# Two blocks' first layer as seven products of parts (Strassen) in an fp32 feed-forward kernel behind a state-space scan

## Chip, cores and metric

The kernel runs on one core of a Trainium2 chip. The metric is the device time of one execution in microseconds. A core has TensorE (matrix products, into PSUM), VectorE, ScalarE and GpSimd (elementwise work) and DMA queues. The profile calls them PE (PEld is its weight load), DVE, ACT and POOL. PSUM has 8 banks of 128 partitions x 512 fp32.

## The reference, cut to what matters

A Mamba2 scan (4 batches, 8 heads, 768 tokens, head size 32) makes y; y is laid out as 3072 tokens x 256, and a feed-forward layer with ELU follows. All is fp32.

```python
x = attn_out.transpose(0, 2, 1, 3).reshape(B * S, H * D)   # 3072 x 256
h = x @ w_in                                                # w_in 256 x 2048
g = np.where(h > 0.0, h, np.exp(np.minimum(h, 0.0)) - 1.0)
return g @ w_out                                            # w_out 2048 x 256
```

## The kernel before

The 3072 tokens are 12 blocks of 256 (`NP = 12`). Block n's scan result stands transposed in `yT[n // 2]`, two blocks in a tile, in two parts of 128 rows (`KC = 2`). `w_in` is cut into 16 column groups of 128 (`MC = 16`). The scan of blocks further on is spread between the products of the feed-forward layer. The instructions of each engine stay in the order of the program (`manual_schedule`); the framework adds the waits and gives out the buffers.

The pools in PSUM: seven banks for everything but the second layer's sums, one bank for those.

```python
p_a = ctx.enter_context(tc.tile_pool(name="ps_a", bufs=7, space=PSUM))
p_o = ctx.enter_context(tc.tile_pool(name="ps_o", bufs=1, space=PSUM))
def psum(shape, name):
    return p_a.tile(shape, F32, tag="a", name=name)
```

A step of the first layer makes two column groups, h of 128 x 2 x 256, with four products. The ELU takes three passes: Relu and Exp on ScalarE, then max(e - 1, h) on VectorE, which also frees the bank.

```python
def l1(n, i):
    if i == 0:
        g_of[n] = ffn.tile([P, MC, BLK], F32, tag="g", name="g", bufs=3)
    ps = psum([P, 2, BLK], "ps_h")
    for j in range(2):
        m = 2 * i + j
        for k in range(KC):
            nc.tensor.matmul(
                out=ps[:, j], lhsT=w_in[:, k, m * P:(m + 1) * P],
                rhs=yT[n // 2][:, k, n % 2].rearrange("p u i -> p (u i)"),
                start=(k == 0), stop=(k == KC - 1))
    lag.append((n, i, ps))

def elu():
    n, i, ps = lag.pop(0)
    e = ffn.tile([P, 2, BLK], F32, tag="e", name="e", bufs=3)
    nc.scalar.activation(e, ps, ACT.Relu, scale=-1.0)
    nc.scalar.activation(e, e, ACT.Exp, scale=-1.0)
    nc.vector.scalar_tensor_tensor(
        out=g_of[n][:, 2 * i:2 * i + 2], in0=e, scalar=1.0, in1=ps,
        op0=ALU.subtract, op1=ALU.max)
```

A step of the second layer, `l2(n, j)`, adds two of the 16 column groups for both halves of the block's tokens, four products as well, into the bank `ps_o` of block n. The last step copies the bank to SBUF with ScalarE and writes it out.

The scan's parts that take PSUM banks from `p_a`: `turn` two (`ps_tb`, `ps_tc`), `scores` four (`ps_g`), which `weigh` reads on VectorE one bank after another; `sums` two (`ps_st`), which `states` reads on VectorE; `across` and `inside` four (`ps_y`), which ScalarE copies into `yT`. `decay` is ScalarE work.

```python
def scores(*ns):
    gs = [psum([P, len(ns), 2, 2, Q], "ps_g") for _ in range(4)]
    # ... 32 products a block; gs[q] for q = 0..3 in turn

def sums(*ns, pool=p_a, tag="a", parts=(None, None)):
    ps = [psum([P, len(ns), 2, 2 * D], "ps_st"),
          pool.tile([P, len(ns), 2, 2 * D], F32, tag=tag, name="ps_st")]
    # ... 16 products a block
```

The loop from block 2 on, cut:

```python
ends = {(3, 14): 4, (5, 8): 6, (7, 13): 8, (9, 6): 10}
def end_of_two(n, step):
    m = ends.get((n, step))
    if m:
        inside(across(m, m + 1), m, m + 1)

for n in range(2, NP):
    for i in range(8):
        l2(n - 2, i)
        # ... conversion of further weights while there are any
        end_of_two(n, 2 * i)
        l1(n, i)
        while lag:
            elu()
        # ... scan of block 3
        m = n + 2 - n % 2
        if 4 <= m < NP and n % 2 == 0:
            # ... loads; decay (i >= 2); turn, turn_exp (i == 5, 7)
        if 4 <= m < NP and n % 2 == 1:
            # ... scaled (i == 0), decay (i < 2)
            if i == (1 if m in (6, 10) else 2):
                scores(m, m + 1)
                sums(m, m + 1)
                for q in range(4):
                    weigh(m, q)
                    weigh(m + 1, q)
                states(m)
                states(m + 1)
        end_of_two(n, 2 * i + 1)
for i in range(8):
    l2(NP - 2, i)
l2_last(NP - 1)
```

Of the kernel before, what the change touches and what calls it, by code (L numbers as in the profile page):

```python
# [10 lines left out]
F32 = mybir.dt.float32  # L11
# [17 lines left out]
def kernel(  # L29
# [43 lines left out]
    ffn = ctx.enter_context(tc.tile_pool(name="ffn", bufs=2))  # L73
    conv = ctx.enter_context(tc.tile_pool(name="conv", bufs=2))
    PSUM = bass.MemoryType.PSUM
    p_a = ctx.enter_context(tc.tile_pool(name="ps_a", bufs=7, space=PSUM))
    p_o = ctx.enter_context(tc.tile_pool(name="ps_o", bufs=1, space=PSUM))

    def psum(shape, name):
        return p_a.tile(shape, F32, tag="a", name=name)  # L80
# [21 lines left out]
    def rows_of(n):  # L102
        b, g = place(n)
        return slice(NG * NH * b + g, NG * NH * (b + 1), NG)
# [101 lines left out]

    idle = att.tile([P, P], BF16, tag="M", name="idle", bufs=8)
    nc.vector.memset(idle, 0.0)  # L210
    ps_idle = p_o.tile([P, 4, P], F32, tag="o", name="ps_idle")

    def idle_products(count):
        for _ in range(count):
            nc.tensor.matmul(
                out=ps_idle, lhsT=idle, rhs=idle.unsqueeze(1).to_broadcast([P, 4, P]),
                start=True, stop=True)

    def idle_product(k):

        nc.tensor.matmul(
            out=ps_idle[:, 0:k], lhsT=ident, rhs=ident.unsqueeze(1).to_broadcast([P, k, P]),
            start=True, stop=True)

    idle_products(7)
    ident = const.tile([P, P], F32, name="ident")
    make_identity(nc, ident)

# [28 lines left out]
        out=minus, in0=ident, scalar1=-1.0, scalar2=None, op0=ALU.mult)  # L257


    heads = [const.tile([ROWS, NH, N], F32, name=f"heads{n}") for n in range(2)]  # L260
    heads.append(heads[0])

    def make_heads(n):
        rows, cols = (slice(BH, 2 * BH), slice(BH + NH * n, BH + NH * (n + 1))) if n < 2 else (
            slice(0, ROWS), rows_of(n))
        count = rows.stop - rows.start
        nc.gpsimd.tensor_copy(
            heads[n][rows], ident[rows, cols].unsqueeze(2).to_broadcast([count, NH, N]))

    make_heads(0)  # L270
    make_heads(1)
# [84 lines left out]
    def first_exp(n):  # L356

        ps = psum([P, 2, P], "ps_ec")
        rows = slice(BH, 2 * BH) if n < 2 else slice(0, ROWS)
        nc.tensor.matmul(  # L360
            out=ps, lhsT=heads[n][rows].rearrange("p h n -> p (h n)"),
            rhs=X0 if n < 2 else F[:, 1], start=True, stop=True,
            tile_position=(rows.start, 0))
        st[n]["ec"] = att.tile([P, 2, P], F32, tag="ec", name="ec", bufs=4)
        nc.scalar.copy(out=st[n]["ec"], in_=ps)

# [183 lines left out]
    def inside(y, *ns):  # L550


        for t in range(2):
            if t and ns[0] == 0:
                idle_products(1)
            for at, n in enumerate(ns):
                s = st[n]
                for u in range(2):
                    for v in range(2):
                        toks = slice(Q * v, Q * v + Q)  # L560
                        for q in range(4):
                            h, col = 4 * t + q, (D * q + shift(n, v)) % P
                            nc.tensor.matmul(  # L563
                                out=y[t][v][col:col + D, at, u],
                                lhsT=s["x"][toks, u, D * h:D * (h + 1)],
                                rhs=s["M"][h // 2][toks, u, h % 2], start=False, stop=True,
                                tile_position=(Q * v, col), skip_group_check=True)
            n = ns[0]
            if n // 2 not in yT:
                yT[n // 2] = ffn.tile([P, KC, 2, 2, P], F32, tag="yT", name="yT")  # L570
            out = yT[n // 2][:, t, n % 2:n % 2 + len(ns)]
            for v in range(2):
                k = shift(n, v)
                for at in (0, k) if k else (0,):
                    count, src = P - k, (at + k) % P
                    to, src = out[at:at + count, :, :, Q * v:Q * v + Q], y[t][v][src:src + count]
                    if t and n == 1:
                        nc.vector.tensor_copy(to, src)
                    else:
                        nc.scalar.copy(out=to, in_=src)  # L580
        for n in ns:
            st.pop(n)
# [3 lines left out]

    def l1(n, i):

        if i == 0:
            g_of[n] = ffn.tile([P, MC, BLK], F32, tag="g", name="g", bufs=3)  # L590
        ps = psum([P, 2, BLK], "ps_h")
        for j in range(2):
            m = 2 * i + j
# [6 lines that stand above are left out]

    lag = []

    def elu():

        n, i, ps = lag.pop(0)
        e = ffn.tile([P, 2, BLK], F32, tag="e", name="e", bufs=3)
        nc.scalar.activation(e, ps, ACT.Relu, scale=-1.0)  # L607
        nc.scalar.activation(e, e, ACT.Exp, scale=-1.0)  # L608
        nc.vector.scalar_tensor_tensor(  # L609
            out=g_of[n][:, 2 * i:2 * i + 2], in0=e, scalar=1.0, in1=ps,  # L610
            op0=ALU.subtract, op1=ALU.max)

    def row_of(n):
        b, g = place(n)
# [4 lines left out]
    def l2(n, j):  # L619


        if j == 0:
            o_of[n] = p_o.tile([P, 2, DM], F32, tag="o", name="ps_o")
        for m in (2 * j, 2 * j + 1):
            for ts in range(2):
                nc.tensor.matmul(  # L626
                    out=o_of[n][:, ts], lhsT=g_of[n][:, m, ts * P:(ts + 1) * P],
                    rhs=w_out[:, m], start=(m == 0 and ts == 0), stop=(m == MC - 1),
                    skip_group_check=True)
        if j == MC // 2 - 1:  # L630
            ob = ffn.tile([P, 2, DM], F32, tag="ob", name="ob")
            nc.scalar.copy(out=ob, in_=o_of.pop(n))  # L632
            r0 = row_of(n)
            nc.sync.dma_start(
                out=out[r0:r0 + BLK, :].rearrange("(t p) e -> p t e", p=P), in_=ob)

    def l2_last(n):

        for ts in range(2):
            ps = psum([P, DM], "ps_o")  # L640
            for m in range(MC):
                nc.tensor.matmul(  # L642
                    out=ps, lhsT=g_of[n][:, m, ts * P:(ts + 1) * P], rhs=w_out[:, m],
                    start=(m == 0), stop=(m == MC - 1))
            ob = ffn.tile([P, 2, DM], F32, tag="ob", name="ob")
            nc.scalar.copy(out=ob[:, ts], in_=ps)
            r0 = row_of(n) + ts * P
            nc.sync.dma_start(out=out[r0:r0 + P, :], in_=ob[:, ts])
# [50 lines left out]
    w_abs(1)  # L699
    kept = st[0]  # L700
    inside(across(0), 0)
    idle_product(3)
    w_low(1, nc.scalar)

    w_sign(1)
# [96 lines left out]
    def end_of_two(n, step):  # L802
        m = ends.get((n, step))
        if m:
            inside(across(m, m + 1), m, m + 1)


    for n in range(2, NP):
        for i in range(8):
            l2(n - 2, i)  # L810
            if todo < len(pieces):
# [9 lines left out]
            if n == 2:  # L821
# [11 lines left out]
                if i == 4:  # L833
                    sums(3)
                    states(3)
            if n == 2 and i == 6:
                inside(across(3), 3)

            m = n + 2 + n % 2
            if 4 < m < NP and n % 2 == 1 and i in (4, 5):  # L840
                spread_cum(m + i - 4)
            m = n + 2 - n % 2
            if 4 <= m < NP and n % 2 == 0:
                if i < 2:
                    if m == 4:
                        spread_cum(m + i)
                    load_bc(m + i)
                    spread_exp(m + i)
                if i == 2:
                    load_x(m)  # L850
                    load_x(m + 1)
                if i >= 2:
                    decay(m + i // 6, (i - 2) % 4)
                if i in (5, 7):
                    turn(m + i // 7)
                    turn_exp(m + i // 7)
            if 4 <= m < NP and n % 2 == 1:
                if i == 0:
                    scaled(m, nc.gpsimd)
                    scaled(m + 1, nc.gpsimd)  # L860
                if i < 2:
                    decay(m + 1, i + 2)
                if i == (1 if m in (6, 10) else 2):
                    scores(m, m + 1)
                    sums(m, m + 1)
                    for q in range(4):
                        weigh(m, q)
                        weigh(m + 1, q)
                    states(m)
                    states(m + 1)  # L870
            end_of_two(n, 2 * i + 1)
    for i in range(8):
        l2(NP - 2, i)
    l2_last(NP - 1)
# [30 lines left out]
```

## Time and profile before

| | |
|---|---|
| device time, median of 3 | 387.46 us (387.11 to 388.42) |
| span of the profiled execution | 385.5 us |
| TensorE busy | 380.4 us |
| ScalarE busy | 197.1 us |
| VectorE busy | 142.7 us |
| GpSimd busy | 73.8 us |
| first layer, `l1` (L595) | 768 records, 181.9 us |
| second layer, `l2` (L626) and `l2_last` (L642) | 704 and 64 records, 166.0 and 14.0 us |

The page gives first the busy time of each engine, then the chain of work that ended last, then the groups of instructions: line, engine and operation, output and inputs, shapes, count, busy time and mean duration of one, and the idle time of the engine just before them with what ended it. A timeline row is start, duration, engine, line, operation and count; rows of one kind that follow each other are merged. The durations of pipelined matmuls overlap, so the price of one is the distance between starts.

### The profile page before, as it was taken

The page shows a single profiled execution, that of the slowest core. Times are in us where ns is not written, and L with a number is a line of the kernel's source. Part 1 is how long each engine was busy: PE and PEld are TensorE (multiplying, and loading weights), DVE is VectorE, ACT ScalarE, POOL GpSimd, SP SyncE. Part 2 cuts the span into 40 slices and gives each one's busy share as a digit, 9 for nine tenths or more (in the row PEclk, how much of TensorE's full clock was granted, in tenths as well). Part 3 has the DMA queues.
Part 4 walks back from the last instruction along what each step waited for, and adds up shares of the span by engine and source line. Part 5 has one row for each costly group of instructions (what it writes and reads, how often), then busy time and mean ns, then how long its engine had stood idle before and what let it go on. Part 6 is the DMA issues. An engine that isn't in the chain of part 4 may idle for free.

```text
span 385.5 us, 8722 instructions
## 1 busy us (share of the span) xinstructions
PE 380.4 (99%) x3568; PEld 324.5 (84%) x3568; DVE 142.7 (37%) x289; ACT 197.1 (51%) x458; POOL 73.8 (19%) x134
## 2 busy tenths in 40 slices
PE   8999999999999999999999999999999999999996
PEld 5668888888888888888888888888888888888885
DVE  3989978932511232611133431124422212221000
ACT  4859969675344576344467335367444333334000
POOL 4554527624100112300022120011310000000000
PEclk9999999999999999999999999999999999999999
DMA  8968987555014505003425001640000000000000
GB/s 170 220 162 208 242 202 146 92 103 111 2 28 55 84 2 136 3 3 61 65 38 130 10 0 35 68 66 29 2 4 0 27 2 26 1 2 28 2 27 27
DMA packets 96248, 25.24 MB, mean 65 GB/s; under 512 B 77328, under 2 KB 92112, under 8 KB 96208
## 3 DMA queue, kind: packets, MB, share of 16 engines
q1 hardware_dynamic: 94032, 24.49, 30.7%
q8 instruction: 28, 0.46, 0.5%
q10 hardware_dynamic: 2176, 0.20, 0.4%
q14 instruction: 12, 0.10, 0.1%
HBM read 21.33 MB, written 3.34 MB: 64 GB/s over the span
## 4 chain that ended last, share of the span: by engine, by line
PE 93%; DVE 4%; ACT 1%; POOL 1%; DMA 1%; issue 0%; ACTq 0%; DVEq 0%; POOLq 0%
PE ps_h L595 41%; PE ps_o L626 40%; PE ps_o L642 4%; PE ps_y L563 2%; PE ps_g L467 2%; PE ps_y L542 1%; PE ps_st L497 1%; DVE mag L183 1%; DVE mag L190 1%; PE ps_tb L382 1%; PE ps_tc L382 1%; DMA la<-in_a_dram 1%; DVE M L476 1%; DVE sgn L175 0%; DVE F L281 0%; POOL w_in L200 0%
## 5 line engine op out<-in xcount | busy, mean ns | idle before, releaser
L595 PE MATMUL ps_h<-yT,w_in 128*128 128x256 f32 x768 | 181.9, 381 | 0.8 <-DVE sgn L175 0.4
L626 PE MATMUL ps_o<-w_out,g 128*128 128x256 f32 x704 | 166.0, 380 | 0.0
L595 PEld LDWEIGHTS ps_h<-yT,w_in 128*128 128x128 f32 x768 | 144.8, 190 | 22.9 <-POOL w_in L200 1.9
L626 PEld LDWEIGHTS ps_o<-w_out,g 128*128 128x128 f32 x704 | 132.4, 190 | 18.1 <-POOL L L452 0.2
L609 DVE SCALAR_TENSOR_TENSOR g<-e,ps_h 128x512 f32<-128x512 f32 x96 | 65.7, 686 | 203.5 <-ACT e L608 203.5
L607 ACT ACTIVATE e<-ps_h 128x512 f32<-128x512 f32 x96 | 57.0, 594 | 134.3 <-PE ps_h L595 130.1
L608 ACT ACTIVATE e<-e 128x512 f32<-128x512 f32 x96 | 60.5, 630 | 3.1
L452 POOL TENSOR_SCALAR_AFFINE_SELECT L<-L 64x512 f32<-64x512 f32 x40 | 27.3, 684 | 158.4 <-ACT L L447 157.1
L447 ACT ACTIVATE L<-L,ncum 128x64 f32<-128x64 f32 x160 | 42.1, 332 | 0.3 <-DMA L<-flat 0.3
L580 ACT COPY yT<-ps_y 64x256 f32<-64x256 f32 (+3 forms) x43 | 13.6, 321 | 11.7 <-PE ps_y L563 11.2
L476 DVE TENSOR_TENSOR M<-ps_g,L 128x256 f32<-128x256 f32 x48 | 17.0, 415 | 0.4 <-PE ps_g L467 0.3
L519 POOL TENSOR_TENSOR Sx<-S_new,hmask 128x64 f32<-128x64 f32 x44 | 12.8, 302 | 17.0 <-DVE S_new L514 11.9
L632 ACT COPY ob<-ps_o 128x512 f32<-128x512 f32 x11 | 6.4, 578 | 15.3 <-PE ps_o L626 15.3
L642 PE MATMUL ps_o<-w_out,g 128*128 128x256 f32 x64 | 14.0, 379 | 0.0
L200 POOL TENSOR_TENSOR w_in<-mag,w_in 128x512 uint32<-128x512 uint32 (+1 forms) x9 | 11.3, 1253 | 13.6 <-DVE mag L190 10.6
L642 PEld LDWEIGHTS ps_o<-w_out,g 128*128 128x128 f32 x64 | 12.2, 190 | 1.7
L200 POOL TENSOR_TENSOR w_out<-mag,w_out 128x512 uint32<-128x512 uint32 x8 | 10.2, 1276 | 14.4 <-DVE mag L190 14.4
L190 DVE SCALAR_TENSOR_TENSOR mag<-mag,sgn 128x512 uint32<-128x512 uint32 (+1 forms) x17 | 12.3, 722 | 0.6
L157 ACT ACTIVATE mag<-w 128x512 f32<-128x512 f32 x16 | 10.8, 676 | 1.9 <-POOL w_in L200 0.9
L514 DVE SCALAR_TENSOR_TENSOR S_new<-S_new,ec,ps_st 128x64 f32<-128x64 f32 x40 | 10.9, 279 | 2.0
L183 DVE TENSOR_SCALAR mag<-mag 128x512 f32<-128x512 f32 (+1 forms) x17 | 10.3, 606 | 1.0 <-ACT mag L157 1.0
L563 PE MATMUL ps_y<-M,xr 64*32 64x64 f32 x768 | 9.8, 225 | 0.0
(74 smaller groups left out, 141.7 us busy)
## 6 DMA issues: line engine op xcount, KB each, us to landing
L<-flat SPq DMA_DIRECT2D x20, 256.0 KB, 5.0
w<-in_moe_w_in_dram SPq DMA_DIRECT2D x8, 512.0 KB, 5.3
w<-in_moe_w_out_dram SPq DMA_DIRECT2D x8, 512.0 KB, 5.8
xr<-in_x_dram SPq DMA_DIRECT2D x24, 128.0 KB, 3.5
out_dram<-ob SPq DMA_DIRECT2D x11, 256.0 KB, 2.2
bc<-in_B_dram SPq DMA_DIRECT2D x24, 64.0 KB, 3.5
bc<-in_C_dram SPq DMA_DIRECT2D x22, 64.0 KB, 2.9
ec<-flat_exp SPq DMA_DIRECT2D x72, 16.0 KB, 1.7
```

What stands on the lines that cost most here:

```text
L190: nc.vector.scalar_tensor_tensor(out=mag, in0=mag, scalar=3, in1=sgn, op0=ALU.logical_shift_left, op1=ALU.bitwise_xor)
L200: nc.gpsimd.tensor_tensor(out=w, in0=w_mag[i][:, :, cols], in1=w, op=ALU.add)
L447: nc.scalar.activation(L[:, h, u], L[:, h, u], ACT.Exp, bias=ncum[:, u, row:row + 1])
L452: nc.gpsimd.affine_select(out=part, in_=part, pattern=[[0, 4], [0, 2], [1, Q]], compare_op=ALU.is_ge, fill=0.0, base=0, channel_multiplier=-1)
L476: nc.vector.tensor_tensor(out=M, in0=s["g"][q], in1=s["L"][:, 2 * q:2 * q + 2].rearrange("p k u i -> p u k i"), op=ALU.mult)
L563: nc.tensor.matmul(out=y[t][v][col:col + D, at, u], lhsT=s["x"][toks, u, D * h:D * (h + 1)], rhs=s["M"][h // 2][toks, u, h % 2], start=Fal ...
L595: nc.tensor.matmul(out=ps[:, j], lhsT=w_in[:, k, m * P:(m + 1) * P], rhs=yT[n // 2][:, k, n % 2].rearrange("p u i -> p (u i)"), start=(k = ...
L607: nc.scalar.activation(e, ps, ACT.Relu, scale=-1.0)
L608: nc.scalar.activation(e, e, ACT.Exp, scale=-1.0)
L609: nc.vector.scalar_tensor_tensor(out=g_of[n][:, 2 * i:2 * i + 2], in0=e, scalar=1.0, in1=ps, op0=ALU.subtract, op1=ALU.max)
L626: nc.tensor.matmul(out=o_of[n][:, ts], lhsT=g_of[n][:, m, ts * P:(ts + 1) * P], rhs=w_out[:, m], start=(m == 0 and ts == 0), stop=(m == MC ...
L642: nc.tensor.matmul(out=ps, lhsT=g_of[n][:, m, ts * P:(ts + 1) * P], rhs=w_out[:, m], start=(m == 0), stop=(m == MC - 1))
```

## The change

From block 4 on, two blocks n and n + 1 go together. For them and two column groups of `w_in` the first layer is a product of a 2 x 2 matrix of parts (128 x 128 of `w_in`) with a 2 x 2 matrix of parts (128 x 256 of `yT`). Done part by part that takes eight products. Strassen's algorithm, here in the form with fifteen sums, takes seven, with sums of weight parts, of input parts and of results around them. The aim is one product less on TensorE for each of the 32 steps (four pairs of blocks, eight steps each).

The sums of weight parts are made once on GpSimd during block 3 (`sum_weights`), those of the inputs once for each pair on GpSimd (`sum_y`). A step is cut in two: `front` makes four products and, after a copy by ScalarE, three sums on VectorE; `back` adds three products into the same two PSUM banks, and VectorE adds once to each bank. The result is h of both blocks in `c1` and `c2`, and the ELU follows for each. Between `front` and `back`, and ahead of `front`, stands one step of the second layer: steps of blocks n - 2 and n - 1 alternate, so two banks hold second-layer sums, and the pool of the others has six.

```diff
-    p_a = ctx.enter_context(tc.tile_pool(name="ps_a", bufs=7, space=PSUM))
-    p_o = ctx.enter_context(tc.tile_pool(name="ps_o", bufs=1, space=PSUM))
+    p_a = ctx.enter_context(tc.tile_pool(name="ps_a", bufs=6, space=PSUM))
+    p_o = ctx.enter_context(tc.tile_pool(name="ps_o", bufs=2, space=PSUM))
...
+    def begin_elu():
+        begun.append(ffn.tile([P, 2, BLK], F32, tag="e", name="e", bufs=3))
+        nc.scalar.activation(begun[0], lag[0][2], ACT.Relu, scale=-1.0)
...
+    def front(n, i):
+        c1, c2 = psum([P, 2, BLK], "ps_h"), psum([P, 2, BLK], "ps_h")
+        s1, s2, s3, s4 = (w[:, i] for w in w_sums)
+        t = y_sums[n]
+        part_product(c1[:, 0], a11[:, i], yT[n // 2][:, 0, 0].rearrange("p u i -> p (u i)"), True)
+        part_product(c2[:, 1], s2, t[:, 1], True)
+        part_product(c2[:, 0], s1, t[:, 0])
+        part_product(c1[:, 1], s3, t[:, 2])
+
+        copy = conv.tile([P, BLK], F32, tag="sgn", name="p_copy")
+        nc.scalar.copy(out=copy, in_=c1[:, 0])
+        u = conv.tile([P, 2, BLK], F32, tag="mag", name="u_sum")
+        nc.vector.tensor_tensor(out=u[:, 0], in0=c2[:, 1], in1=copy, op=ALU.add)
+        nc.vector.tensor_tensor(out=u[:, 1], in0=c2[:, 0], in1=u[:, 0], op=ALU.add)
+        nc.vector.tensor_tensor(out=c2[:, 1], in0=c1[:, 1], in1=u[:, 1], op=ALU.add)
+        open_[n, i] = c1, c2, u
+
+    def back(n, i):
+        c1, c2, u = open_.pop((n, i))
+        b21, b22 = (yT[n // 2][:, 1, at].rearrange("p u i -> p (u i)") for at in range(2))
+        part_product(c1[:, 0], a12[:, i], b21)
+        part_product(c1[:, 1], a22[:, i], y_sums[n][:, 3])
+        part_product(c2[:, 0], w_sums[3][:, i], b22)
+        nc.vector.tensor_tensor(out=c1[:, 1], in0=c1[:, 1], in1=u[:, 0], op=ALU.add)
+        nc.vector.tensor_tensor(out=c2[:, 0], in0=c2[:, 0], in1=u[:, 0], op=ALU.add)
+        lag.append((n, i, c1))
+        lag.append((n + 1, i, c2))
...
-    for n in range(2, NP):
+    for n in (2, 3):
         # ... as before, with sum_weights(i) in block 3
+    for n in range(4, NP, 2):
+        for k in range(16):
+            l2(n - 2 + k % 2, k // 2)
+            at = n + k // 8
+            end_of_two(at, 2 * (k % 8))
+            if k % 2 == 0:
+                front(n, k // 2)
+            else:
+                back(n, k // 2)
+            if lag:
+                elu()
+            if lag:
+                begin_elu()
+            scan_ahead(at, k % 8)
+            end_of_two(at, 2 * (k % 8) + 1)
+    while lag:
+        elu()
```

`elu` takes up a Relu that `begin_elu` has issued. `scan_ahead` is the part of the old loop that works on the scan of the next blocks, unchanged. `end_of_two` also calls `sum_y(m)`. The outputs g get 24 small buffers for three large ones.

Smaller edits go with it. The products on zeros that fill TensorE at the start are fp32, one over 4 x 128 and one over 3 x 128 columns, in place of seven in bf16 over 512; two such fillings further on, one inside the first `inside` and one behind it, are gone. `heads` and the product in `first_exp` take all 128 rows for the first two blocks where they took 32.

More of the change, by code (lines that the diff above doesn't have):

```diff
@@ L205 @@
     w_load(0)
-    idle = att.tile([P, P], BF16, tag="M", name="idle", bufs=8)
+    idle = att.tile([P, P], F32, tag="M", name="idle", bufs=8)
     nc.vector.memset(idle, 0.0)
     ps_idle = p_o.tile([P, 4, P], F32, tag="o", name="ps_idle")
[L213 to L217, printed above, removed]
     def idle_product(k):
         nc.tensor.matmul(
-            out=ps_idle[:, 0:k], lhsT=ident, rhs=ident.unsqueeze(1).to_broadcast([P, k, P]),
+            out=ps_idle[:, 0:k], lhsT=idle, rhs=idle.unsqueeze(1).to_broadcast([P, k, P]),
             start=True, stop=True)
-    idle_products(7)
+    idle_product(4)
+    idle_product(3)
     ident = const.tile([P, P], F32, name="ident")
@@ L257 @@
         out=minus, in0=ident, scalar1=-1.0, scalar2=None, op0=ALU.mult)
-    heads = [const.tile([ROWS, NH, N], F32, name=f"heads{n}") for n in range(2)]
+    heads = [const.tile([P, NH, N], F32, name=f"heads{n}") for n in range(2)]
     heads.append(heads[0])
     def make_heads(n):
-        rows, cols = (slice(BH, 2 * BH), slice(BH + NH * n, BH + NH * (n + 1))) if n < 2 else (
-            slice(0, ROWS), rows_of(n))
-        count = rows.stop - rows.start
+        cols = slice(BH + NH * n, BH + NH * (n + 1)) if n < 2 else rows_of(n)
         nc.gpsimd.tensor_copy(
-            heads[n][rows], ident[rows, cols].unsqueeze(2).to_broadcast([count, NH, N]))
+            heads[n], ident[:, cols].unsqueeze(2).to_broadcast([P, NH, N]))
     make_heads(0)
@@ L358, in first_exp @@
         ps = psum([P, 2, P], "ps_ec")
-        rows = slice(BH, 2 * BH) if n < 2 else slice(0, ROWS)
+        rows = P if n < 2 else ROWS
         nc.tensor.matmul(
-            out=ps, lhsT=heads[n][rows].rearrange("p h n -> p (h n)"),
-            rhs=X0 if n < 2 else F[:, 1], start=True, stop=True,
-            tile_position=(rows.start, 0))
+            out=ps, lhsT=heads[n][0:rows].rearrange("p h n -> p (h n)"),
+            rhs=la0 if n < 2 else F[:, 1], start=True, stop=True)
         st[n]["ec"] = att.tile([P, 2, P], F32, tag="ec", name="ec", bufs=4)
@@ L553, in inside @@
         for t in range(2):
-            if t and ns[0] == 0:
-                idle_products(1)
             for at, n in enumerate(ns):
@@ L587, in l1 @@
     def l1(n, i):
-        if i == 0:
-            g_of[n] = ffn.tile([P, MC, BLK], F32, tag="g", name="g", bufs=3)
         ps = psum([P, 2, BLK], "ps_h")
@@ L601 @@
     lag = []
+    begun = []
+    def begin_elu():
+        begun.append(ffn.tile([P, 2, BLK], F32, tag="e", name="e", bufs=3))
+        nc.scalar.activation(begun[0], lag[0][2], ACT.Relu, scale=-1.0)
     def elu():
+        if not begun:
+            begin_elu()
         n, i, ps = lag.pop(0)
-        e = ffn.tile([P, 2, BLK], F32, tag="e", name="e", bufs=3)
-        nc.scalar.activation(e, ps, ACT.Relu, scale=-1.0)
+        e = begun.pop()
         nc.scalar.activation(e, e, ACT.Exp, scale=-1.0)
+        g_of[n, i] = ffn.tile([P, 2, BLK], F32, tag="g", name="g", bufs=24)
@@ L609, in elu, with sum_weights @@
         nc.vector.scalar_tensor_tensor(
-            out=g_of[n][:, 2 * i:2 * i + 2], in0=e, scalar=1.0, in1=ps,
+            out=g_of[n, i], in0=e, scalar=1.0, in1=ps,
             op0=ALU.subtract, op1=ALU.max)
+    w_parts = w_in.rearrange("p k (i r c) -> p k r i c", r=2, c=P)
+    a11, a12, a21, a22 = (w_parts[:, k, r] for r in range(2) for k in range(2))
+    w_sums = []
+    def sum_weights(step):
+        r, part = step // 2, slice(4 * (step % 2), 4 * (step % 2) + 4)
+        if step % 2 == 0:
+            w_sums.append(conv.tile([P, MC // 2, P], F32, tag="w64", name="w_sum", bufs=W_AHEAD))
+        in0, in1, op = (
+            (a21, a22, ALU.add), (w_sums[0], a11, ALU.subtract),
+            (a11, a21, ALU.subtract), (a12, w_sums[min(r, 1)], ALU.subtract))[r]
+        nc.gpsimd.tensor_tensor(out=w_sums[r][:, part], in0=in0[:, part], in1=in1[:, part], op=op)
@@ new lines, with sum_y, part_product @@
+    y_sums = {}
+    def sum_y(n):
+        t = y_sums[n] = conv.tile([P, 4, BLK], F32, tag="w64", name="y_sum", bufs=W_AHEAD)
+        b11, b12, b21, b22 = (
+            yT[n // 2][:, k, at].rearrange("p u i -> p (u i)") for k in range(2) for at in range(2))
+        for r, (in0, in1) in enumerate(((b12, b11), (b22, t[:, 0]), (b22, b12), (b21, t[:, 1]))):
+            nc.gpsimd.tensor_tensor(out=t[:, r], in0=in0, in1=in1, op=ALU.subtract)
+    open_ = {}
+    def part_product(out, lhsT, rhs, first=False):
+        nc.tensor.matmul(
+            out=out, lhsT=lhsT, rhs=rhs, start=first, stop=True, skip_group_check=True)
@@ L626, in l2 @@
                 nc.tensor.matmul(
-                    out=o_of[n][:, ts], lhsT=g_of[n][:, m, ts * P:(ts + 1) * P],
+                    out=o_of[n][:, ts], lhsT=g_of[n, j][:, m % 2, ts * P:(ts + 1) * P],
                     rhs=w_out[:, m], start=(m == 0 and ts == 0), stop=(m == MC - 1),
@@ L642, in l2_last @@
                 nc.tensor.matmul(
-                    out=ps, lhsT=g_of[n][:, m, ts * P:(ts + 1) * P], rhs=w_out[:, m],
+                    out=ps, lhsT=g_of[n, m // 2][:, m % 2, ts * P:(ts + 1) * P], rhs=w_out[:, m],
                     start=(m == 0), stop=(m == MC - 1))
@@ L701 @@
     inside(across(0), 0)
-    idle_product(3)
     w_low(1, nc.scalar)
@@ L805, in end_of_two, with scan_ahead @@
             inside(across(m, m + 1), m, m + 1)
-    for n in range(2, NP):
+            sum_y(m)
+    def scan_ahead(n, i):
+        m = n + 2 + n % 2
+        if 4 < m < NP and n % 2 == 1 and i in (4, 5):
+            spread_cum(m + i - 4)
+        m = n + 2 - n % 2
+        if 4 <= m < NP and n % 2 == 0:
+            if i < 2:
+                if m == 4:
+                    spread_cum(m + i)
+                load_bc(m + i)
+                spread_exp(m + i)
+            if i == 2:
+                load_x(m)
+                load_x(m + 1)
+            if i >= 2:
+                decay(m + i // 6, (i - 2) % 4)
+            if i in (5, 7):
+                turn(m + i // 7)
+                turn_exp(m + i // 7)
+        if 4 <= m < NP and n % 2 == 1:
+            if i == 0:
+                scaled(m, nc.gpsimd)
+                scaled(m + 1, nc.gpsimd)
+            if i < 2:
+                decay(m + 1, i + 2)
+            if i == (1 if m in (6, 10) else 2):
+                scores(m, m + 1)
+                sums(m, m + 1)
+                for q in range(4):
+                    weigh(m, q)
+                    weigh(m + 1, q)
+                states(m)
+                states(m + 1)
+    for n in (2, 3):
         for i in range(8):
@@ L835 @@
                     states(3)
[L836 to L870, printed above, removed]
-            end_of_two(n, 2 * i + 1)
+                if i == 6:
+                    inside(across(3), 3)
+            else:
+                sum_weights(i)
+            scan_ahead(n, i)
+            end_of_two(n, 2 * i + 1)
+    for n in range(4, NP, 2):
[5 more added lines that the diff above has]
+                front(n, k // 2)
+            else:
+                back(n, k // 2)
+            if lag:
+                elu()
+            if lag:
+                begin_elu()
+            scan_ahead(at, k % 8)
+            end_of_two(at, 2 * (k % 8) + 1)
+    while lag:
+        elu()
     for i in range(8):
```

## The prediction

> **What bounds the kernel now.** I read the page's busy shares first, then the chain that ended last, then the groups by shape, and at last the timeline of single stages.
>
> ```profile
> PE 380.4 (99%) x3568; PEld 324.5 (84%) x3568; DVE 142.7 (37%) x289; ACT 197.1 (51%) x458; POOL 73.8 (19%) x134
> ...
> PE 93%; DVE 4%; ACT 1%; POOL 1%; DMA 1%; issue 0%; ACTq 0%; DVEq 0%; POOLq 0%
> ```
>
> The chain says the same as the busy share: TensorE sets the time, so a product removed shortens the span, and a hole opened in TensorE lengthens it. The other engines have room on average. Now the rows that price the parts (records, busy us, mean ns):
>
> ```profile
> L595 PE MATMUL ps_h<-yT,w_in 128*128 128x256 f32 x768 | 181.9, 381 | 0.8 <-DVE sgn L175 0.4 <-POOL w_in L200 0.2
> L626 PE MATMUL ps_o<-w_out,g 128*128 128x256 f32 x704 | 166.0, 380 | 0.0
> ...
> L476 DVE TENSOR_TENSOR M<-ps_g,L 128x256 f32<-128x256 f32 x48 | 17.0, 415 | 0.4 <-PE ps_g L467 0.3
> ...
> L580 ACT COPY yT<-ps_y 128x256 f32<-128x256 f32 x8 | 3.0, 373 | 5.5 <-PE ps_y L563 5.4
> ```
>
> The code issues 12 x 32 = 384 first-layer products and the row has 768 records: one fp32 product is two records. The 381 ns is a record's latency, not its price. The price is the pitch, seen in the timeline of one stage:
>
> ```profile
> 156.49 1.89 PE L595 MATMUL ps_h<-yT,w_in 128*128 128x256 f32 x8
> ...
> 158.22 1.89 PE L626 MATMUL ps_o<-w_out,g 128*128 128x256 f32 x8
> 158.42 0.60 ACT L607 ACTIVATE e<-ps_h 128x512 f32<-128x512 f32 x1 [3.36 <-PE ps_h L595]
> 159.04 0.63 ACT L608 ACTIVATE e<-e 128x512 f32<-128x512 f32 x1
> ```
>
> Eight records start 158.22 - 156.49 = 1.73 us apart from the next eight: **0.43 us for one product**. ScalarE's Relu starts 0.20 us after the next group began, so a reader of a group's last product starts 0.20 us behind the end of its stream.
>
> **What the skill says.**
> - PSUM — Partial Sum Buffer, "PSUM bank collisions raise a hardware error": two engines may not be in one bank and quadrant at once, even at different columns; guard by bank. No run here shows a collision. The compiled program of the kernel before does guard so: the first copy out of ps_st reads only the first chunk, yet waits for the count that the third chunk raises, which is the next write to that bank.
> - TensorE: Matmul & The Clock Gate, "Step-by-step: what each phase is for": LDWEIGHTS are pulled ahead of running matmuls. The trace agrees (load rows start 0.2 us before their matmuls). A wait sits on the load, so a late one also shows a load: the record after a wait for w_in takes 483 ns where 379 is usual, 0.10 us more.
> - VectorE: DVE Perf Modes, "The DRAIN you can't avoid": a read of what the operation before wrote needs a semaphore. The timeline has such a pair, and 0.04 us between them:
>
> ```profile
> 13.82 0.94 DVE L183 TENSOR_SCALAR mag<-mag 128x512 f32<-128x512 f32 x1
> 14.80 0.69 DVE L190 SCALAR_TENSOR_TENSOR mag<-mag,sgn 128x512 uint32<-128x512 uint32 x1
> ```
>
> - Perfetto Trace Analysis, "Optimization Strategy": the same gap repeating on the engine that should be full can mean that PSUM ran out. The kernel before has no such gaps from 97 us on (TensorE's load queue waits 2.8 us in all from there to 357 us).
>
> **Part 1, the product saved.** Four pairs of blocks, eight steps each, 7 products for 8: 32 x 0.43 = **13.8 us less**.
>
> **Part 2, the sums between `front` and `back`.** In a step, TensorE runs second layer (4 products, 1.73), `front` (4, 1.73), second layer (1.73), `back` (3, 1.29). `back`'s first product writes bank c1, so it waits for VectorE's last read of c1, the third sum. The copy out of c1 in turn waits for the fourth product of `front`, since that one writes the other half of c1 (by bank, as above). From the end of `front`'s stream: 0.20 until the copy starts, 0.37 copy, 0.03 to VectorE, three sums that each need the one before, 3 x 0.415 + 2 x 0.04 = 1.33, and 0.06 to TensorE: 1.99 us. The second layer between covers 1.73. The hole is 0.26, and with the exposed load **0.36 us a step**. Three of the 32 steps have other TensorE work there (scores, or a pair's end): 29 x 0.36 = **10.5 us more**. So a step gains 0.43 and loses 0.36.
>
> I checked that the copy isn't also late by its queue: after `back`, ScalarE has Relu, exp, Relu (to 2.0 us behind `back`'s end) and at most 1.05 us of decays and a 0.36 us copy, done by 3.45; `front`'s copy is due at 3.65.
>
> **Part 3, six PSUM buffers for seven.** The scores take four, the state sums two, a first-layer product still in the ELU one. In the kernel before that is just seven, and the timeline shows no wait:
>
> ```profile
> 152.74 1.21 PE L467 MATMUL ps_g<-ctm,bt 32*64 32x128 f32 x64
> ...
> 153.87 0.86 PE L497 MATMUL ps_st<-xr,sc 64*32 64x64 f32 x64
> 154.13 0.69 DVE L609 SCALAR_TENSOR_TENSOR g<-e,ps_h 128x512 f32<-128x512 f32 x1 [2.76 <-ACT e L608]
> 154.66 1.99 PE L626 MATMUL ps_o<-w_out,g 128*128 128x256 f32 x8
> ```
>
> One of the seven goes over to the second-layer pool, and two open buffers, c1 and c2, come in. The first-layer group before it began at 150.91, so its stream ended at 152.64; scores and sums end 2.02 later, at 154.66, and the ELU's g 2.2 later, at 154.82. By place, counted from the end of the products ahead of the scores:
> - Block 3, scores for 4 and 5: the second sum buffer waits for that g, 2.2 - 1.2 = 1.0 us.
> - Pairs 4 and 8 (step k = 9, behind `back`): c1 and c2 are both in the ELU. The scores get four; the sums' first buffer comes with g at 2.2, the second after two weighings at 3.0. The sums then end at 3.9 in place of 2.0: 1.9 us each, 3.8.
> - Pair 6 (k = 10, behind `front`): c1, c2 open, and the odd block's c2 still held until its g, which stands behind copy and sums, at 2.65. The fourth score bank waits for it; scores end at 3.95, two pairs of weighings (0.75, 0.7) free the two sum banks, sums end at 6.4 in place of 2.0: 4.4.
> - Pair ends: at k = 14 of pair 6 the four ps_y want a fourth buffer that comes at 2.65: 2.7 with the load; at k = 11 of pair 8 the same, of which the second layer covers 1.73: 1.0.
> Sum **12.9 us more**. This is the part I am least sure of, since buffers come free in an order that I worked out by hand.
>
> **Part 4, the start and the rest.** With six buffers the first block's tc and the fourth score bank wait for earlier readers (0.2 and about 0.5): 0.7 us, in a stage where VectorE is busy 9.9 of 10 us, so it stays. The warm-up products keep their length in columns; those removed lie in waits. Sums of weights and of inputs go to GpSimd: 8 of 128x512 at 1.3 and 16 of 128x256 at 0.67, 21 us in a stretch where it is idle. VectorE gains 160 sums x 0.415 = 66 us, 143 to 209 of some 390; ScalarE 32 x 0.37 = 12. None becomes the bound.
>
> **Sum.** 387.5 - 13.8 + 10.5 + 12.9 + 0.7 = 397.8. I take 396, since waits in Part 3 may swallow holes of Part 2.
>
> **Rivals.**
> 1. *The saving comes through.* If the copy may start behind the first product, the sums hide under `front`, Part 2 falls away, and the time is about 387; if the buffers also come free sooner than I worked out, 375 to 380. For it: low busy shares of VectorE and ScalarE, and an order of products in `front` that is the order of use. Against it: the waits by bank in the compiled program.
> 2. *VectorE becomes the bound.* A step asks of it 5 x 0.415 + 2 x 0.69 = 3.45 us in 6.5. Only near the weighings (8 x 0.34 and 8 sums of states at 0.33 more, 5.4 us) is it full; then a hole per pair of 1 to 2 us, some 4 us, is on top: 400.
> 3. *The start pays.* Fewer warm-up products let the granted clock fall early. The page has 1.00 throughout, with TensorE busy over 9 of 10 us; I give it 1 us at most.
>
> **Range and chances.** Part 2's hole is 0.26 between two numbers near 1.9, so plus or minus 0.1 us a step, 3 us. Part 3 may be off by 5. Together, with rival 1 as a tail towards faster: 384 to 402. The line of 2% slower is at 395.2, just below my number; that of 2% faster, 379.7, needs both halves of rival 1.
>
> **What would show it.** Right: a repeating wait of TensorE's load of `back`'s first product on VectorE's sum, about 0.26 us, 29 times; waits of score, sum and ps_y products on g and on the weighings, some us each, once or twice a pair; TensorE with 64 records fewer and busy share down to about 93%. Wrong: `front`'s copy starting under `front`'s own products; `back` following the second layer without a gap; pair steps of 6.47 us in place of 6.83. The prediction falls first if the waits by bank don't hold for c1, or if scan work lies in other gaps than I placed it.

## The result and the profile after

The changed kernel takes **406.0 us** (median; 405.25 to 407.38) against 387.28 in the same runs: ratio 1.048, 95% interval 1.044 to 1.053. It is slower, as forecast, but by 18.7 us, where 8.5 were forecast, and outside the range that ended at 402.

The page of the changed kernel, busy shares and chain, answers to the two lines shown of before:

```profile
span 403.5 us, 8811 instructions
...
PE 376.7 (93%) x3498; PEld 312.3 (77%) x3498; DVE 209.1 (52%) x449; ACT 202.1 (50%) x490; POOL 95.1 (24%) x158
...
PE 72%; DVE 12%; ACT 10%; issue 4%; POOL 1%; DMA 1%; DVEq 0%; ACTq 0%; POOLq 0%
```

TensorE has less to do (3498 records for 3568: 64 are the products saved, 6 the fillings) and yet the span is longer: for 27 us of it TensorE does not work (5 before). Of the chain, 93% were TensorE; now 22% are VectorE and ScalarE, the engines that it waits for. The waits of TensorE's load queue in the pair stage (120 to 375 us; in all, times, longest) say for what:

```profile
PEld ps_h L644 <- issue: 11.1, 17, 0.7
PEld ps_h L644 <- ACT L L439: 7.8, 12, 0.7
PEld ps_st L489 <- issue: 5.3, 6, 1.4
PEld ps_y L534 <- DVE g L605: 3.0, 2, 2.4
PEld ps_g L459 <- DVE g L605: 2.4, 1, 2.4
```

L644 is the product of parts: 17 + 12 = 29 waits, one for each step in which only the second layer stands between `front` and `back`. The releasers in these two rows mislead ("issue", a decay on ScalarE): `back` waits for two semaphores, and the last that the page sees is not the one that counts. The rows below, ps_g, ps_y and ps_st, are the scan's products that wait for a bank. The timeline of one step shows what the 29 wait for:

```profile
320.09 1.89 PE L690 MATMUL ps_o<-w_out,g 128*128 128x256 f32 x8
320.29 0.37 ACT L658 COPY p_copy<-ps_h 128x256 f32<-128x256 f32 x1 [1.68 <-PE ps_h L644]
...
320.69 0.43 DVE L660 TENSOR_TENSOR u_sum<-ps_h,p_copy 128x256 f32<-128x256 f32 x1 [1.85 <-ACT p_copy L658]
321.15 0.42 DVE L661 TENSOR_TENSOR u_sum<-ps_h,u_sum 128x256 f32<-128x256 f32 x1
321.68 0.43 DVE L662 TENSOR_TENSOR ps_h<-ps_h,u_sum 128x256 f32<-128x256 f32 x1
...
322.26 0.67 PE L644 MATMUL ps_h<-yT,w_in 128*128 128x256 f32 x2 [0.28 <-DVE ps_h L662]
```

`front`'s stream ends at 320.09, where the second layer begins; copy and three sums end at 322.11; the second layer's stream ends at 321.81. Two records of `back` then take 0.67 us where two in a row take 0.59. From step to step (315.26 to 322.26, the starts of `back`) it is 7.00 us; 15 products are 6.47, so the hole is **0.52 us**, and the 6.90 us that the old way takes for 16 products was better.

Where the 18 us of span arise, by comparing when the same second-layer product starts in both traces: +2.8 us before the first one of block 0 (53.29 to 56.11), +0.9 up to the first of block 2, where the pair stage begins (117.23 to 120.99), then +2.4 in pair 4, +8.5 in pair 6, +2.7 in pair 8 and +0.7 in pair 10.

### The profile page after: what moved, and what is told of

The parts are those of the page before. It is cut to its first block, busy times and chain, and to the rows that moved or that the text cites. A ratio compares the mean times of both kernels' runs of the same rounds, so it can differ in the third digit from the quotient of the medians.

```text
span 403.5 us, 8811 instructions
## 1 busy us (share of the span) xinstructions
PE 376.7 (93%) x3498; PEld 312.3 (77%) x3498; DVE 209.1 (52%) x449; ACT 202.1 (50%) x490; POOL 95.1 (24%) x158
## 4 chain that ended last, share of the span: by engine, by line
PE 72%; DVE 12%; ACT 10%; issue 4%; POOL 1%; DMA 1%; DVEq 0%; ACTq 0%; POOLq 0%
PE ps_h L644 25%; PE ps_o L690 25%; PE ps_h L583 11%; PE ps_o L706 3%; ACT L L439 3%; ACT p_copy L658 2%; ACT e L603 2%; DVE ps_h L662 2%; DVE u_sum L660 2%; DVE u_sum L661 2%; PE ps_y L553 2%; PE ps_y L534 1%; DVE g L605 1%; ACT e L596 1%; DVE M L468 1%
## 5 line engine op out<-in xcount | busy, mean ns | idle before, releaser
L690 PE MATMUL ps_o<-w_out,g 128*128 128x256 f32 x704 | 167.2, 382 | 0.0
L583 PE MATMUL ps_h<-yT,w_in 128*128 128x256 f32 x256 | 60.6, 382 | 3.0 <-issue 1.1
L583 PEld LDWEIGHTS ps_h<-yT,w_in 128*128 128x128 f32 x256 | 47.8, 190 | 10.9 <-POOL w_in L200 1.5
L644 PE MATMUL ps_h<-yT,w_in 128*128 128x256 f32 x128 | 40.5, 398 | 8.2 <-DVE ps_h L662 4.8
L644 PE MATMUL ps_h<-y_sum,w_sum 128*128 128x256 f32 x192 | 46.7, 379 | 0.0
L660 DVE TENSOR_TENSOR u_sum<-ps_h,p_copy 128x256 f32<-128x256 f32 x32 | 13.6, 425 | 55.2 <-ACT p_copy L658 55.2
L644 PEld LDWEIGHTS ps_h<-y_sum,w_sum 128*128 128x128 f32 x192 | 36.5, 190 | 5.0
L644 PEld LDWEIGHTS ps_h<-yT,w_in 128*128 128x128 f32 x128 | 21.8, 189 | 20.9 <-issue 11.1
L658 ACT COPY p_copy<-ps_h 128x256 f32<-128x256 f32 x32 | 11.9, 372 | 47.8 <-PE ps_h L644 47.8
L672 DVE TENSOR_TENSOR ps_h<-ps_h,u_sum 128x256 f32<-128x256 f32 x32 | 13.9, 433 | 30.8 <-PE ps_h L644 30.8
L644 PE MATMUL ps_h<-yT,w_sum 128*128 128x256 f32 x64 | 19.0, 379 | 0.0
L644 PE MATMUL ps_h<-y_sum,w_in 128*128 128x256 f32 x64 | 19.0, 379 | 0.0
L662 DVE TENSOR_TENSOR ps_h<-ps_h,u_sum 128x256 f32<-128x256 f32 x32 | 13.9, 433 | 3.3
```

The costliest lines, as they stand in the source:

```text
L583: nc.tensor.matmul(out=ps[:, j], lhsT=w_in[:, k, m * P:(m + 1) * P], rhs=yT[n // 2][:, k, n % 2].rearrange("p u i -> p (u i)"), start=(k = ...
L644: nc.tensor.matmul(out=out, lhsT=lhsT, rhs=rhs, start=first, stop=True, skip_group_check=True)
L658: nc.scalar.copy(out=copy, in_=c1[:, 0])
L660: nc.vector.tensor_tensor(out=u[:, 0], in0=c2[:, 1], in1=copy, op=ALU.add)
L662: nc.vector.tensor_tensor(out=c2[:, 1], in0=c1[:, 1], in1=u[:, 1], op=ALU.add)
L690: nc.tensor.matmul(out=o_of[n][:, ts], lhsT=g_of[n, j][:, m % 2, ts * P:(ts + 1) * P], rhs=w_out[:, m], start=(m == 0 and ts == 0), stop=( ...
```

## The experiments

The theory after the trace: the saving is real, and three things eat it, **the chain through bank c1**, **the lack of banks**, and in pair 6 **a fall of the granted clock**. Rivals: VectorE is too full, or the edits of the start cost something. In the expectations "block 2's second layer" means the first second-layer product in the loop of block 2, at 53.29 us in the kernel before.

### e1: the kernel before with six banks

```diff
-    p_a = ctx.enter_context(tc.tile_pool(name="ps_a", bufs=7, space=PSUM))
-    p_o = ctx.enter_context(tc.tile_pool(name="ps_o", bufs=1, space=PSUM))
+    p_a = ctx.enter_context(tc.tile_pool(name="ps_a", bufs=6, space=PSUM))
+    p_o = ctx.enter_context(tc.tile_pool(name="ps_o", bufs=2, space=PSUM))
```

> The kernel before with six banks for everything and two for the second layer, nothing else. If the banks are what delays the start, block 2's second layer begins 2.8 us later than before (53.29 us to about 56.1), and each of the four scores of a pair of blocks waits 0.9 to 1.0 us more for the ELU's g: 2.8 + 4 x 0.95 = 6.6, so about 394 us. If the edits of the start are what delays it, only the four waits are left: about 391 us.

Measured: 396.74 us, ratio 1.025 (1.022 to 1.027). The first second-layer product starts at 57.59, 4.3 us late, more than expected. Each of the four scores of a pair waits; here the one of blocks 4 and 5, as TensorE's timeline has it:

```profile
100.95 0.32 PE L497 MATMUL ps_st<-xr,sc 64*32 64x64 f32 x8
101.21 0.69 DVE L609 SCALAR_TENSOR_TENSOR g<-e,ps_h 128x512 f32<-128x512 f32 x1 [2.77 <-ACT e L608]
...
101.95 0.66 PE L497 MATMUL ps_st<-xr,sc 64*32 64x64 f32 x40 [0.69 <-DVE g L609]
```

Four products (8 records) go into the first sum bank, then TensorE stands until the ELU's g, done at 101.90, gives the seventh tile's bank back. One bank less costs the old kernel 9.4 us by itself. Some 1.7 us of the delay at the start come as early as 14 to 16 us, where a first-layer product of block 0 waits 2.4 us; the trace doesn't name for what.

### e2: the kernel before with the start of the changed one

The edits are those of the diff above on `idle`, `idle_product`, `heads` and `first_exp`; seven banks stay.

> The kernel before with the changed kernel's start alone (fp32 filling products, two fillings left out, 128 rows in the first exp product), seven banks. If the banks delay the start, nothing is seen here: 387.3 us within 0.6. If the edits or the clock behind them delay it: about 390 us, with block 2's second layer at 56 us in place of 53.3.

Measured: 386.79 us, ratio 0.9989 (0.9981 to 0.9998). The edits do no harm to the time; that first second-layer product is even 0.8 us earlier (52.49). The delay at the start is the banks'.

### e3: the products into c1 ahead of those into c2

```diff
         part_product(c1[:, 0], a11[:, i], ..., True)
+        part_product(c1[:, 1], s3, t[:, 2])
         part_product(c2[:, 1], s2, t[:, 1], True)
         part_product(c2[:, 0], s1, t[:, 0])
-        part_product(c1[:, 1], s3, t[:, 2])
```

> The changed kernel with the two products into c1 ahead of the two into c2 in front; the same products and sums. Waits by bank: the copy may start behind the second product, 0.86 us earlier, and the first sum then waits for the fourth product instead of the copy. The chain from front's end is 0.20 + 0.43 + 0.03 + 0.42 + 0.10 + 0.43 + 0.1, about 1.7 us against 1.73 of second layer: the hole of 0.52 us falls to about 0.1, 28 times 0.4 is 11 us less, about 395 us. Rival, VectorE or the second layer's own banks make the hole: it stays and so does the time, 406 us.

Measured: 392.69 us, ratio 1.014 (1.011 to 1.018); 13.3 us less than the changed kernel with the same products, copies and sums. A step of e3's timeline:

```profile
349.66 0.37 ACT L658 COPY p_copy<-ps_h 128x256 f32<-128x256 f32 x1 [0.81 <-PE ps_h L644]
...
350.32 1.89 PE L690 MATMUL ps_o<-w_out,g 128*128 128x256 f32 x8
350.59 0.42 DVE L660 TENSOR_TENSOR u_sum<-ps_h,p_copy 128x256 f32<-128x256 f32 x1 [1.51 <-ACT e L603]
...
352.09 0.67 PE L644 MATMUL ps_h<-yT,w_in 128*128 128x256 f32 x2
```

The copy now starts 0.66 us before `front`'s stream ends (350.32), just behind the second product. In both kernels it reads what the first product wrote; in the changed one it started only behind the fourth, the other one into that bank. So the wait is by bank, and not only for the half that is read; as c1 is one tile that fills one bank, a wait by tile would look the same. The step is 6.59 us (345.50 to 352.09), the hole 0.11.

### e5: four sums, none of which reads c1 late

```diff
-        nc.vector.tensor_tensor(out=u[:, 0], in0=c2[:, 1], in1=copy, op=ALU.add)
-        nc.vector.tensor_tensor(out=u[:, 1], in0=c2[:, 0], in1=u[:, 0], op=ALU.add)
-        nc.vector.tensor_tensor(out=c2[:, 1], in0=c1[:, 1], in1=u[:, 1], op=ALU.add)
+        nc.vector.tensor_tensor(out=u[:, 1], in0=c1[:, 1], in1=copy, op=ALU.add)
+        nc.vector.tensor_tensor(out=u[:, 0], in0=c2[:, 1], in1=copy, op=ALU.add)
+        nc.vector.tensor_tensor(out=u[:, 1], in0=c2[:, 0], in1=u[:, 1], op=ALU.add)
+        nc.vector.tensor_tensor(out=c2[:, 1], in0=c2[:, 1], in1=u[:, 1], op=ALU.add)
```

> The order of e3, and the third sum split so that nothing of c1 is read late: c1[1] + copy first, then the sums with c2; four sums for three. back's first product then waits for nothing that is late. If the chain through bank c1 is the whole of the hole, a pair step falls from 6.99 (e3: 6.59) to 6.47 us, as many as its 15 products take, 3.5 us below e3: about 389 us. If VectorE, which gets 32 x 0.43 = 14 us more, is close to a bound: no better than e3's 392.7 us.

Measured: 389.96 us, ratio 1.007 (1.004 to 1.009). In e5's timeline the one sum that reads c1 (L660) starts while `front` still runs and is done 0.17 us into the second layer's 1.73, and `back` follows on the second layer without a gap:

```profile
347.10 0.42 DVE L660 TENSOR_TENSOR u_sum<-ps_h,p_copy 128x256 f32<-128x256 f32 x1 [0.98 <-ACT p_copy L658]
...
347.35 1.89 PE L691 MATMUL ps_o<-w_out,g 128*128 128x256 f32 x8
347.55 0.42 DVE L661 TENSOR_TENSOR u_sum<-ps_h,p_copy 128x256 f32<-128x256 f32 x1
...
349.08 0.59 PE L644 MATMUL ps_h<-yT,w_in 128*128 128x256 f32 x2
```

347.35 to 349.08 is 1.73, the second layer and nothing else. Over pair 10 e5 gains 3.45 us on the kernel before, 8 x 0.43: the saving in full, while VectorE does more (217 us busy for 209). So VectorE's load was not the matter; the order on it was. The whole kernel is still slower than before, for the waits for banks and for falls of the clock: its mean granted clock was 0.986 in four of five executions, and the fifth, at 0.994, took 388.02 us.

### e4: the odd block's ELU ahead of `front`

```diff
             if k % 2 == 0:
+                if lag:
+                    elu()
                 front(n, k // 2)
```

> The changed kernel with the odd block's exp and g issued ahead of front's copy and sums instead of behind them. If the wait for a PSUM bank held by that g is the cause: the 2.40 us in the scores of blocks 8 and 9, the 2.43 us in their ps_y and the 0.71 us in those of 10 and 11 go (5.5 us), and with the scores' wait the fall of the granted clock (some 2.2 us): 398 us; 400.5 us if the clock still falls. If the banks are held by something else: 406 us.

Measured: 399.82 us, ratio 1.032 (1.030 to 1.034), 6.2 less than the changed kernel. TensorE's timeline at the scores of blocks 8 and 9, first the changed kernel, then e4:

```profile
223.47 0.44 PE L459 MATMUL ps_g<-ctm,bt 32*64 32x128 f32 x6
...
226.04 1.89 PE L459 MATMUL ps_g<-ctm,bt 32*64 32x128 f32 x58 [2.13 <-DVE g L605]
```

```profile
224.38 0.44 PE L459 MATMUL ps_g<-ctm,bt 32*64 32x128 f32 x6
225.06 1.16 PE L459 MATMUL ps_g<-ctm,bt 32*64 32x128 f32 x58 [0.24 <-DVE g L605]
...
227.28 0.32 PE L489 MATMUL ps_st<-xr,sc 64*32 64x64 f32 x8 [1.07 <-DVE M L468]
```

Six records are three products, three banks; the fourth bank was held by g. With g early that wait shrinks from 2.1 to 0.2 us, and both waits of ps_y for g are gone. The wait of the state sums for the weighings (M) stays. A fall of the clock stayed too in the profiled execution, but at the scores of blocks 10 and 11; the other three had a mean clock of 0.999 to 1.000 and took 399.6 to 399.9 us, more than the 398 expected without a fall. A part of that is a new cost: the two holes behind the scores of pair 4, where VectorE also has the weighings and the states, grow from 0.28 us of idle TensorE each to 0.78 and 1.16, now that g stands ahead of `front`'s sums.

### e9: e5 and e4 together

> e5 and e4 together, scores, state sums and pair ends where the changed kernel has them. If the hole and the banks held by g are separate costs, the gains add: 406.0 - 16.0 - 6.2 = 383.8 us, and what e6 has beyond that (3 us) is the move of the state sums. If one hides the other, e.g. a filled hole lets the waits for banks grow, it is 387 us or more.

Measured: 385.88 us, ratio 0.996 (0.994 to 0.997), with an unusual spread, 383.78 to 387.85 over ten executions. It goes with the granted clock: 383.8 us at a mean of 1.000, 384.6 to 386.2 at 0.995 to 0.996, 386.4 to 387.3 at 0.991, 387.9 at 0.987. The one execution without a fall meets the 383.8 expected. That the gains add exactly isn't shown by it, since the 406.0 and the 16.0 it was worked out from are medians of executions with falls in them.

### e6: the state sums one step later

e9, with `scores` at i = 2 for all pairs, `sums` and `states` at i = 3, and other places for the pair ends:

```diff
-ends = {(3, 14): 4, (5, 8): 6, (7, 13): 8, (9, 6): 10}
+ends = {(3, 14): 4, (5, 10): 6, (7, 10): 8, (9, 10): 10}
-            if i == (1 if m in (6, 10) else 2):
+            if i == 2:
                 scores(m, m + 1)
-                sums(m, m + 1)
                 # ... weigh as before
-                states(m)
-                states(m + 1)
+            if i == 3 and m > 4:
+                sums(m, m + 1)
+                states(m)
+                states(m + 1)
```

(For m = 4, in block 3, all stays at i = 2.)

> e5 with e4's early ELU, the state sums of the pairs 6, 8 and 10 moved one step behind their scores (after back, where the weighings have given the banks back), scores of all three at the same step, and the pair ends ahead of a back with c1, c2 open. Theory: the waits for banks of the pair stage (1.9 + 4.2 + 2.4 + 1.9 + 0.7) and the fall of the clock (2) go, of the 13.8 us saved all but the start's 2.8 and block 3's 0.9 are kept: about 377 us. Rival, the waits only move to other products, as buffers are short in any order: 385 us or more.

Measured: 380.79 us, ratio 0.984 (0.982 to 0.986), 3.8 us above what was expected. The clock was granted in full in all executions. By the starts of the same second-layer products, the four pairs save 10.5 us on the kernel before, 3.3 less than the 13.8 of the products. Three things move at once here, so what each of them is worth isn't shown.

### e8 and e7: seven banks where there is no pair

One bank of the second layer comes from the common pool, from block 3 on:

```diff
-            o_of[n] = p_o.tile([P, 2, DM], F32, tag="o", name="ps_o")
+            o_of[n] = psum([P, 2, DM], "ps_o") if n > 2 and n % 2 else p_o.tile(
+                [P, 2, DM], F32, tag="o", name="ps_o")
```

with `bufs=7` for `ps_a` and `bufs=1` for `ps_o`. e8 is the changed kernel with this, e7 is e6 with this.

> The changed kernel with that same giving out of banks and nothing else. If the six banks cost only in the blocks before the pair stage, 406 - 3.6 - 0.9 = 401.5 us with block 2's second layer at 52.5 us; the pair stage has the same banks as in the changed kernel and keeps its waits. Rival, the start's waits have another cause: 406 us.

> e6 with seven banks in the common pool and one for the second layer; the second layer's other bank is taken from the common pool from block 3 on. The blocks before the pair stage then have what they had in the kernel before: 3.6 us at the start and 0.9 us at block 3's scores less than e6, about 373 us; by the count of products alone 387.3 - 13.8 = 373.5.

Measured: e8 400.95 us, ratio 1.036 (1.034 to 1.038), 5.05 less than the changed kernel. e7 **375.73 us**, ratio 0.972 (0.969 to 0.974): faster than both kernels by clear margins, and 5.1 less than e6, where 4.5 was expected; the 373 are missed by what e6 missed. The waits of e7's load queue in its pair stage (116 to 350 us):

```profile
PEld ps_g L459 <- DVE g L605: 1.4, 3, 0.5
PEld ps_st L489 <- issue: 1.0, 3, 0.3
PEld ps_y L534 <- issue: 1.0, 3, 0.3
PEld ps_g L459 <- issue: 1.0, 3, 0.3
```

No product of parts is among them, and no wait is over half a microsecond.

## Why the prediction was wrong

Most of its mechanisms were there; two sizes were too small, and one cost was missing. Of the 8.2 us between its sum, 397.8, and 406.0, the size of the hole makes 4.6, the start 2.1 and the clock some 2.1; Part 3 gives 1.0 back; 0.4 stays open.

- **Part 1 (13.8 us saved): right.** e5's steps give 0.43 us each once nothing stands in the way.
- **Part 2 (the hole): right in cause, the size is the term that failed.** 29 holes were forecast and 29 are in the trace, but of 0.52 us, not 0.36: 15.1 us for 10.5. The term 3 x 0.415 + 2 x 0.04 was 1.33 and measured 1.42 (320.69 to 322.11), since the sum into PSUM takes 0.43 and starts 0.11 behind the one before, where 0.04 had been taken from another pair; then 0.12 us pass before `back`'s load (322.23), for 0.06. Both places wait for two semaphores. The hole is the difference of two numbers near 2, so 0.15 us of small things made it nearly half as large again.
- **Part 3 (12.9 us): right.** By the traces block 3 has 0.9 (forecast 1.0), the scores of pairs 4 and 8 wait 1.8 each (1.9), of pair 6 4.3 (4.4), the ps_y 2.4 and 0.7 (2.7 and 1.0): 11.9. e1, e4 and e6 show that it is the banks.
- **Part 4 (the start, 0.7): wrong in place and size.** The first block, where the wait was forecast, reaches its first layer 0.6 us sooner (12.74 for 13.33). The loss comes in blocks 1 and 2, at 30 to 54 us, where first-layer tiles meet scores, state sums and ps_y; the prediction named no wait there. At 53 us it is 2.8 us, and 3.4 against e7, which has seven banks there and the same start.
- **Left out: the clock.** Rival 3 looked for it at the start. In the profiled execution it fell in pair 6, at a wait of 2.1 us. The stretches of the changed kernel, with PEclk the number ahead of the last two:

```profile
224.00:226.00 2.00, 0.00 (x0) 0.00 (x0) 1.85 (x4) 0.47 (x1) 0.31 (x1) 1.00 0.00 0
226.00:228.00 2.00, 1.89 (x58) 1.49 (x58) 0.01 (x1) 0.00 (x0) 0.00 (x0) 0.55 0.03 8
228.00:230.00 2.00, 0.88 (x42) 0.70 (x43) 2.00 (x7) 0.00 (x0) 0.00 (x0) 0.50 0.00 0
230.00:232.00 2.00, 2.00 (x47) 1.60 (x28) 1.81 (x8) 0.00 (x0) 0.87 (x3) 0.50 0.00 0
```

TensorE stands for 2 us, then runs at half the clock for nearly 7. Pair 6 is 8.5 us longer; its waits are 6.7, and its eight steps, two of them without a hole, come to -0.3: some 2.1 us are left for the clock, an estimate. Rival 3 isn't out either: in the profiled executions of e8 and e9, which have the changed kernel's start, the clock also fell at 14.1 and 14.4 us, behind a stop of 0.9 us that the changed kernel's own trace has too, without a fall. The eight records of block 0's first step took 3.29 and 3.27 us where they take 2.33 in the changed kernel's trace, 1 us as rival 3 had it. Two of the changed kernel's four executions had a lower mean clock than the profiled one (0.987 for 0.992); where it fell there is not on record.

The sum with measured terms: 387.3 - 13.8 + 15.1 + 11.9 + 2.8 + 2.1 = 405.4, against 406.0 measured and 405.25 in the profiled execution. Taking 396 for the 397.8 of my own sum, because waits might swallow holes, was the wrong way too: the three steps without a hole were already left out of the 29.

Rival 1 fell with e3: the copy waited for the bank. Rival 2 fell with e5: more work on VectorE, and a faster kernel.

## What to carry to other kernels

Where reads and writes of a bank exclude each other, plan products and sums by banks: finish one bank before the other is begun, and let the next product into a bank depend only on the sum that is done first. A change that takes products off a full TensorE has to pay for its open tiles: count the banks in use at every place where other work takes several at once, and free the oldest first, by issuing its reader ahead of the new chain. Here those three orders (e5, e4, e6) and a bank lent only while it is needed (e7) made 375.7 us of 406.0 with the same seven products for eight.

## What was not expected of the hardware

- The granted clock fell to half at waits that aren't long. In the changed kernel it fell where TensorE stood for 2.1 us at the scores of pair 6, and stayed full where it stood for 2.2 us soon after (245.8 to 248.0, ps_y of the same pair), and at the scores of pairs 4 and 8, where the load queue waited 1.4 and 0.4 us; in e4 and e9 it did fall behind waits like these last in the profiled execution. In e9 each 0.0045 of mean clock goes with about 1.3 us, by a line through its ten executions. That the waits bring the falls is read from where most of them lie, and from e6 and e7, which have neither long waits nor, in seven of their eight executions, a mean clock under 0.999. It is not shown: waits of one length went both ways, and in e2, where the start alone was changed, two of 20 executions had 0.995. What decides in a given execution stays open.
- The load of a product that waits for two semaphores started 0.12 us behind the sum that ended last (322.11 to 322.23); the one wait priced from the kernel before was 0.06.
